# Decode attention with a Mish layer on one core: who issues the loads

## The chip, the cores and the metric

The kernel runs on one core of a Trainium2 chip. A core has a matrix engine (TensorE, PE), a vector engine (VectorE, DVE), an activation engine (ScalarE, ACT), a general engine (GpSimd, POOL) and a synchronising engine (SyncE, SP). Each runs its own stream of instructions; they wait for one another through semaphores. 16 DMA engines move data between the memory of the chip (HBM) and the on-chip memory (SBUF). PE writes to a second on-chip memory, PSUM.

The metric is the time of one execution on the device, in microseconds (us), as the median of several runs.

## The reference

For 8 batches with one new token each, a layer-normalised row goes through two branches, which are added to the input: attention over a cache of 8192 keys and values, with 32 query heads that share 8 key/value heads, and a dense layer with a Mish activation.

```python
xn = _layernorm(x, axis=-1)                               # x: 8 x 1 x 512
q = (xn @ wq).reshape(B, Sq, 32, 128).transpose(0, 2, 1, 3)
k = jnp.repeat(k_cache, 4, axis=1)                        # caches: 8 x 8 x 8192 x 128
v = jnp.repeat(v_cache, 4, axis=1)
p = _softmax(einsum("bhqd,bhkd->bhqk", q, k) * 128 ** -0.5)
a = einsum("bhqk,bhkd->bhqd", p, v).transpose(0, 2, 1, 3).reshape(B, Sq, 4096) @ wo
h = xn @ w1 + b1                                          # w1: 512 x 1792
sp = log1p(exp(-abs(h))) + where(h > 0, h, 0)
return x + a + (h * tanh(sp)) @ w2                        # w2: 1792 x 512
```

All data is float32. The two caches are 268 MB each, and each of their bytes is used once.

## The kernel before

The work is cut into 16 packs. A pack is two batches and two key/value heads. For each of its two batches the kernel loads one block of keys and one of values, 128 partitions by 64 KB, 8.39 MB each. So there are 32 K loads and 32 V loads (two V loads are cut into two pieces each). Beside them stand the weights: four loads of `wq`, three of `wo` and a last one in two parts, one of `w1`, and `w2` in three parts at the end. That makes 79 loads.

The loads go into three places in SBUF. `kva` holds V blocks (and at the start `w1` and the second K block), `kvb` holds K blocks (at the end a V block and `w2`), `kvw` holds `wq` or `wo`. `kvb` is a quarter larger than one block: two successive K blocks lie a quarter apart, and the 16 rounds of score matmuls run forward for one block and backward for the next. So the next K load overlaps only three quarters of the old block, and waits for 48 of its 64 matmuls.

For each batch of a pack, PE multiplies the queries with the K block (tile `c`, 64 matmuls), ACT copies the scores out of PSUM (`sc`), and PE gathers them by rows (`s`). After the second batch DVE takes the row maxima, ACT the exponentials, and DVE transposes and folds them into the weights `pt`. While the scores of pack p are worked on, PE multiplies the weights of pack p-1 with its V blocks (tile `o`, 64 matmuls), and DVE gathers the result (`os`).

The program is written once as a list of operations (class `Program`); who waits for whom is derived from the tiles that operations read and write. Each ordered pair of producer and consumer has a semaphore, with two further rules. A DMA counts as a producer of its own, named by its `stream` ("k", "v", "w" and so on). And `relay(engine, to, after)` puts a bare wait on an engine's stream that, once passed, tells another engine. PE, DVE and ACT run packs 1 to 15 as a loop; in each round they lower their semaphores again. SP and POOL run straight through.

The loads stand in one queue (`plan`, L499). `pump` (L479) issues from its head as long as the place is free; `release` (L491) frees a place, keeps the relay that tells of its last reader in `held`, and pumps again. All loads are DMAs on SP's stream, in this order: `wq`, `w1`, the first K block; then K and V in turn, with a weight now and then. SP waits for the place to be read, issues, and goes on to the next. PE waits for a load's own semaphore. The relays that tell SP stand on DVE for V blocks and weights (after the matmuls that read them), on ACT for the second K block and on POOL for `w1`. K loads wait for PE itself. All instructions carry line L383 of the code, where a helper records them; they are told apart by their tiles.

At the start POOL sets up an identity matrix and a few constants. After that it has only the relays of `w1`. At the end it clears the semaphores.

Of the kernel before, what the change touches and what calls it, by code (L numbers as in the profile page):

```python
# [59 lines left out]
W2R = G * FT // 2 * FP // P  # L60
FAR = 1e38


ENGINES = ("tensor", "vector", "scalar", "gpsimd", "sync")
LOOPED = ("tensor", "vector", "scalar")
FIRST, END = 1, PACKS
RARE = ("w",)
# [7 lines left out]
class Op:  # L75
    def __init__(self, engine, method, make=None, outs=(), ins=(), stream=None, to=None):
        self.engine, self.method, self.make = engine, method, make
        self.outs, self.ins, self.to = outs, ins, to
        self.who = stream or engine
        self.unit = 16 if stream else 1  # L80
        self.waits = []


class Engine:
# [25 lines left out]
class Program:  # L110
# [74 lines left out]
    def add(self, op, after=()):  # L185
        op.pack, op.seq = self.pack, len(self.ops)
        looped = self.zone == "loop"
        op.part = self.name if looped else None
        if op.who in RARE:
            op.part = op.who  # L190
        key = op.engine, self.zone, self.at if looped else 0
        start = self.starts[self.pack] if looped else 0
        number = self.numbers.get((*key, start), 0)
        self.numbers[(*key, start)] = number + 1
        op.place = (*key, number)
        op.n = self.count.get(op.who, 0)
        self.count[op.who] = op.n + 1
        know = self.know[op.engine]
        op.needs = [*after, *self.conflicts(op)]
        for other in op.needs:  # L200
            if know.get(other.who, -1) < other.n or op.method == "relay":
                giver = self.giver(op, other)
                self.learn(know, giver)
                op.waits.append(giver)
        assert op.who == op.engine or know.get(op.who, -1) == op.n - 1, op.who
        op.clock = dict(know)
        self.ops.append(op)
        if op.to:
            self.sends[op.place] = op.to
        for ap, writes in [(a, False) for a in op.ins] + [(a, True) for a in op.outs]:  # L210
            self.seen[ap.tensor.name][op.who, writes, self.region(ap)] = op
        return op
# [231 lines left out]
def kernel(  # L444
# [13 lines left out]
    prog = Program(nc)  # L458
    pe, dve, act, pool, sp = (getattr(prog, e) for e in ("tensor", "vector", "scalar", "gpsimd", "sync"))
# [13 lines left out]
    taken, landed, held = {}, {}, {}  # L473
# [25 lines left out]
    def plan(what, at, blocks, stream, part=(0, 1), lo=0):  # L499

        rows = rows_of(blocks)
        n = rows.shape[1]
        t = place[at][:, lo : lo + n]

        cols = slice(round(part[0] * n), round(part[1] * n))

        def load():
            sp.dma_start(t[:, cols], rows[:, cols], stream=stream, to="tensor", after=held.pop(at, ()))
            return t

        queue.append((what, at, load))
# [39 lines left out]
    for p in range(PACKS):  # L551
        for b in range(PB):
            plan_k(p, b)
            if (p, b) in between:
                what, i = between[p, b]
# [169 lines left out]
    def queries(w):  # L725

        for r in range(QR):
            for e in range(2):
                last = pe.matmul(
                    H[HE * e : HE * (e + 1), :],  # L730
                    xnT[:, r].rearrange("p g q -> p (g q)"),
                    w[:, r * BW + e * D : r * BW + (e + 1) * D],
                    start=(r == 0),
                    stop=(r == QR - 1),
                )
        read = prog.relay("vector", "sync", last)
        copies = Q * KR // DH
        qs, qt = wide, raw
        for g in range(copies):
            dve.tensor_scalar_mul(  # L740
                qs.rearrange("p (h r g i) -> p h r g i", h=REP, r=KR, g=copies)[:, :, :, g],
                H.rearrange("p (h i r) -> p h r i", h=REP, r=KR),
                DH**-0.5,
            )
        dve.transpose(qt, qs)
        dve.tensor_copy(
            qc,
            qt.rearrange("p (h r q) -> p h r q", h=REP, r=KR)[:, :, :, :B].rearrange(
                "p h r b -> p b r h"
            ),  # L750
        )
        prog.settle("vector")
        return read
# [15 lines left out]
    def scores(b, k, order, first=False):  # L769

        t = qT[:, b].rearrange("p r u h -> p r (u h)")
        for r in order:
            if first and r == order[KR // 2]:
                load_early()
            for c in range(2):
                last = pe.matmul(
                    C[b][HE * c : HE * (c + 1), :],
                    t[:, r],
                    k[:, r * BW + c * 512 : r * BW + (c + 1) * 512],
                    start=(r == order[0]),  # L780
                    stop=(r == order[-1]),
                )
        read = prog.relay("scalar", "sync", last) if first else None
        act.copy(sc, C[b])
        return read

# [152 lines left out]
    def outputs(w):  # L939

        for h in range(2):
            for r in range(OR):
                at = r * BW + h * D
                last = pe.matmul(
                    H[Q * r : Q * r + B, :],
                    oW[:, r, h, :],
                    w[:, at : at + D],
                    start=(h == 0),
                    stop=(h == 1),
                )  # L950
        read = prog.relay("vector", "sync", last)
        dve.tensor_add(acc, H, acc)
        return read

# [25 lines left out]
    def mish(w1_sb):  # L980


        hp = O[1][:, :FG]
        for g in range(G):
            pe.matmul(
                hp[Q * g : Q * g + B, :], gsel[:, g, :], b1_sb, start=True, stop=False
            )
        for r in range(W1R):
            for g in range(G):
                at = r * F // 2 + g % 2 * FG  # L990
                last = pe.matmul(
                    hp[Q * g : Q * g + B, :],
                    xw[:, r, g // 2, :],
                    w1_sb[:, at : at + FG],
                    start=False,
                    stop=(r == W1R - 1),
                )

        read = prog.relay("gpsimd", "sync", last)
        done = prog.relay("gpsimd", "vector", last)  # L1000
        h, a, z, z2 = (wide[:, i * 512 : i * 512 + FG] for i in range(4))
        dve.tensor_copy(h, hp, after=[done])


        dve.scalar_tensor_tensor(a, h, -1.0, h, op0=ALU.mult, op1=ALU.max)
        act.activation(z, a, AF.Exp, scale=-1.0)
        dve.tensor_mul(z2, z, z)
        m = a
        dve.tensor_single_scalar(m, h, 0.0, op=ALU.is_gt)

        one = acc[:, :FG]
        dve.tensor_scalar(one, z2, -1.0, 1.0, op0=ALU.mult, op1=ALU.add)
        dve.tensor_mul(one, one, m)
        t1 = m
        dve.tensor_add(t1, one, z2)
        t2 = z2
        dve.tensor_scalar(one, one, -1.0, 1.0, op0=ALU.mult, op1=ALU.add)
        dve.scalar_tensor_tensor(t2, z, 2.0, t1, op0=ALU.mult, op1=ALU.add)
        dve.scalar_tensor_tensor(t1, one, 2.0, t2, op0=ALU.mult, op1=ALU.add)
        dve.reciprocal(z, t1)  # L1020
        dve.tensor_mul(t1, t2, z)
        got = one
        half = FG // 2
        for e in range(2):
            dve.tensor_mul(
                got.rearrange("p (i a e l) -> p e a l i", a=2, e=2, i=W2R)[:, e],
                h[:, half * e : half * (e + 1)].rearrange("p (a l i) -> p a l i", a=2, i=W2R),
                t1[:, half * e : half * (e + 1)].rearrange("p (a l i) -> p a l i", a=2, i=W2R),
            )
        dve.transpose(aT.rearrange("p j q -> p (j q)"), got)  # L1030
        dve.memset(acc, 0.0)
        dve.tensor_copy(acc[:B, :], x_sb)
        return read
# [19 lines left out]
    read = queries(landed["wq", 0])  # L1053
    release(("wq", 0), read)
    expand(0)
    read = mish(landed["w1"])
    release("w1", read)

    for p in range(PACKS):
        prog.enter(p)  # L1060
        for b in range(PB):
            k = landed.pop(("k", p, b))
            n = PB * p + b - (p > 0)
            order = range(KR) if n % 2 == 0 else range(KR - 1, -1, -1)
            read = scores(b, k, order, first=(p, b) == (0, 1))
# [23 lines left out]
            if (p, b) in between:  # L1089
                w = landed.pop(between[p, b])  # L1090
                read = outputs(w) if b else queries(w)
                release(between[p, b], read)
            prog.part(None)
            if p > 0:
                last = values(b, landed.pop(("v", p - 1, b)))
                read = prog.relay("vector", "sync", last)
                gather(b)
                release(("v", p - 1, b), read)
            if b == 1:
# [9 lines left out]
    collect(2)  # L1109
    turning()  # L1110
    last = values(0, landed["v", p, 0])
    read = prog.relay("vector", "sync", last)
    gather(0)
    release(("v", p, 0), read)
    sums()
# [67 lines left out]
```

## Time and profile before

| | |
|---|---|
| median of 3 runs | 1303.72 us (1303.66 to 1303.83) |
| span of the profiled execution | 1302.2 us |
| what the runs' median has beside that span | 1.5 us |
| moved by DMA | 561.22 MB in 11554 packets |
| busy: PE, DVE, ACT, POOL | 67%, 30%, 9%, 0% |

The profile comes from one execution, whose own time is its span; the runs' median holds in addition what lies before the first and after the last instruction. In the rows an instruction is named by its engine, its operation and its tiles (output <- inputs), with `xN` for a group of N. "PEld" is the loading of weights into PE. "SPq", "POOLq" and "DVEq" are an engine's own sequencer: waits, and the issuing of DMAs. In brackets stands how long the engine had been idle before and what ended that. The chain of waits is followed back from the last instruction: start, duration, and what it was. A row by stage has start and end, length, busy time (and number of instructions) of PE, PEld, DVE, ACT and POOL, the clock granted to PE, the busy share of the 16 DMA engines and GB/s. A row of DMA issues ends with the median of us from issue to landing.

### The profile page before, as it was taken

The numbers are of one execution on the slowest core, as the hardware profiler recorded it, in microseconds if no ns is written. First come the engines' busy times: TensorE is split into PE (matmuls) and PEld (weight loads), VectorE is DVE, ScalarE is ACT, GpSimd is POOL, SyncE is SP. The second block draws the span as 40 slices with busy tenths as digits, with TensorE's granted clock in tenths as the row PEclk, the third lists the DMA queues.
The fourth block names the chain that finished last, engine by engine and source line by source line (L and its number), as shares of the span: only waits on it lengthen the run. The fifth ranks groups of instructions, "written<-read, shape, count | busy, mean of one in ns | idle before, by whom it ended". The sixth has DMA issues, their size and how long they took to land.

```text
span 1302.2 us, 11363 instructions
## 1 busy us (share of the span) xinstructions
PE 869.0 (67%) x4814; PEld 278.5 (21%) x4814; DVE 389.9 (30%) x597; ACT 122.2 (9%) x294; POOL 4.8 (0%) x10
## 2 busy tenths in 40 slices
PE   4786666766567665686656686666866656756568
PEld 1222112212112221122211222111221121212113
DVE  6350504305051230521405132052320515105061
ACT  1020202001020100200102020020100102001020
POOL 1000000000000000000000000000000000000000
PEclk9898789887799788897877897778877888878779
DMA  9999999999999999999999999999999999999998
GB/s 404 447 419 446 421 441 429 431 439 429 439 429 441 425 443 423 436 433 431 439 429 439 420 450 425 441 425 441 429 431 439 429 439 429 441 425 439 427 429 372
DMA packets 11554, 561.22 MB, mean 431 GB/s; under 512 B 1292, under 2 KB 1424, under 8 KB 1688
## 3 DMA queue, kind: packets, MB, share of 16 engines
q1 hardware_dynamic: 11520, 561.06, 99.7%
q8 instruction: 7, 0.11, 0.0%
q10 hardware_dynamic: 24, 0.02, 0.0%
q14 instruction: 3, 0.02, 0.0%
HBM read 561.01 MB, written 0.07 MB: 431 GB/s over the span
## 4 chain that ended last, share of the span: by engine, by line
DMA 61%; PE 31%; DVE 1%; issue 0%; SPq 0%; ACT 0%; DVEq 0%
DMA kvb<-in_kT 60%; PE c L383 29%; DMA kvb<-in_w 2%; PE o L383 1%; DVE raw L383 0%; DVE pt L383 0%; PE h L383 0%; DVE os L383 0%; DVE nm L383 0%; PE s L383 0%; PE m L383 0%; SPq L383 0%; ACT sc L383 0%; DVE acc L383 0%; DVE nr L383 0%
## 5 line engine op out<-in xcount | busy, mean ns | idle before, releaser
L383 PE MATMUL c<-kvb,qT 128*64 128x512 f32 x1984 | 497.7, 665 | 332.8 <-DMA kvb<-in_kT 332.2
L383 PEld LDWEIGHTS c<-kvb,qT 128*64 128x64 f32 x1984 | 160.8, 154 | 669.6 <-issue 459.4
L383 PE MATMUL o<-kva,pt 128*32 128x512 f32 x1984 | 238.0, 635 | 24.5 <-DMA kva<-in_v 24.1
L383 DVE TENSOR_REDUCE nm<-s 128x1 f32<-128x1024 f32 x16 | 19.6, 1225 | 437.0 <-PE s L383 437.0
L383 DVE STREAM_TRANSPOSE raw<-wide 128x2048 f32<-128x2048 f32 x36 | 125.5, 3485 | 19.5 <-ACT wide L383 17.7
L383 ACT COPY sc<-c 128x512 f32<-128x512 f32 x32 | 18.8, 586 | 979.1 <-PE c L383 979.1
L383 PEld LDWEIGHTS o<-kva,pt 128*32 128x32 f32 x1984 | 64.6, 116 | 189.1 <-issue 147.6
L383 ACT ACTIVATE wide<-s,nms 128x512 f32<-128x512 f32 x128 | 88.0, 688 | 130.4 <-DVE nms L383 66.9
L383 DVE TENSOR_TENSOR oT<-m,rt 128x16 f32 (+1 forms) x17 | 3.0, 175 | 229.6 <-PE m L383 229.6
L383 DVE TENSOR_SCALAR os<-o,isel 128x128 f32<-128x128 f32 x32 | 11.2, 350 | 151.1 <-PE o L383 151.1
L383 DVE TENSOR_TENSOR pt<-raw 64x256 f32<-64x256 f32 x128 | 53.6, 418 | 1.9
L383 DVE TENSOR_TENSOR qT<-qc,bsel 128x1024 f32<-128x1024 f32 x34 | 40.2, 1221 | 13.3 <-PE s L383 13.3
L383 PE MATMUL s<-sc,csel 64*128 64x512 f32 x128 | 37.1, 656 | 8.5 <-ACT sc L383 7.1
L383 DVE TENSOR_TENSOR raw<-raw 128x1024 f32<-128x1024 f32 x32 | 39.2, 1225 | 2.9 <-DVE raw L383 0.2
L383 DVE SCALAR_TENSOR_TENSOR os<-o,isel,os 128x128 f32<-128x128 f32 x96 | 33.6, 350 | 3.4
L383 ACT ACTIVATION_READ_ACCUMULATOR wide<-s,nms 128x1 f32 x128 | 24.7, 193 | 0.0
L383 PE MATMUL m<-hsel,os 128*128 128x8 f32 x66 | 12.7, 265 | 10.5 <-DVE lsel L383 10.5
L383 PE MATMUL m<-ident,nm 128*1 128x128 f32 x16 | 4.3, 270 | 21.6 <-DVE nm L383 21.6
L383 PE MATMUL h<-kvw,xnT 128*64 128x512 f32 x64 | 17.6, 700 | 0.0
L383 PE MATMUL c<-kva,qT 128*64 128x512 f32 x64 | 15.7, 652 | 2.1 <-DMA kva<-in_kT 2.1
L383 DVE TENSOR_SCALAR wide<-h 128x512 f32<-128x512 f32 x16 | 11.1, 691 | 19.9 <-PE h L383 19.5
L383 PEld LDWEIGHTS m<-hsel,os 128*128 128x128 f32 x66 | 10.1, 193 | 25.3 <-issue 12.2
(92 smaller groups left out, 162.1 us busy)
## 6 DMA issues: line engine op xcount, KB each, us to landing
kvw<-in_wq SPq DMA_DIRECT2D x4, 2048.0 KB, 30.3
kva<-in_v SPq DMA_DIRECT2D x2, 4096.0 KB, 21.6
kvw<-in_wo SPq DMA_DIRECT2D x3, 2048.0 KB, 30.4
kva<-in_v SPq DMA_DIRECT2D x1, 6144.0 KB, 24.3
kva<-in_w SPq DMA_DIRECT2D x1, 3584.0 KB, 15.8
kva<-in_v SPq DMA_DIRECT2D x1, 2048.0 KB, 28.8
kvb<-in_w SPq DMA_DIRECT2D x1, 2048.0 KB, 13.7
kvw<-in_wo SPq DMA_DIRECT2D x1, 1536.0 KB, 16.9
```

Of the source, the lines that this page charges most:

```text
L383: got = getattr(engine, o.method)(*args, **kw)
```

## The change

The first three loads (`wq`, `w1`, the first K block) stay on SP. The other 76 are issued on POOL's stream (`pool.dma_start`), where GpSimd's software writes the descriptors. Their semaphores go to SP instead of PE. Behind each of them SP gets a relay, the load's `proxy`: a wait for the landing that then tells PE. Whoever would have waited for such a load waits for its proxy. The relays that told SP that a place is free now tell POOL, on the same engines as before; the one for `w1` is left out, as POOL waits for PE's matmul itself.

```diff
+FIRST_LOADS = (("wq", 0), "w1", ("k", 0, 0))
+MORE = {}
...
@@ class Op
+        self.proxy = None
...
@@ Program.add
         for other in op.needs:
             if know.get(other.who, -1) < other.n or op.method == "relay":
+                if other.proxy and op.engine != other.proxy.engine:
+                    other = other.proxy
                 giver = self.giver(op, other)
...
@@ plan
         def load():
-            sp.dma_start(t[:, cols], rows[:, cols], stream=stream, to="tensor", after=held.pop(at, ()))
+            first = what in FIRST_LOADS
+            op = (sp if first else pool).dma_start(
+                t[:, cols],
+                rows[:, cols],
+                stream=stream,
+                to="tensor" if first else "sync",
+                after=held.pop(at, ()),
+                **({} if first else MORE),
+            )
+            if not first:
+                op.proxy = prog.add(Op("sync", "relay", to="tensor"), [op])
+                op.proxy.part = stream if stream in RARE else None
             return t
...
@@ queries, outputs, the body (V blocks)
-        read = prog.relay("vector", "sync", last)
+        read = prog.relay("vector", "gpsimd", last)
...
@@ scores
-        read = prog.relay("scalar", "sync", last) if first else None
+        read = prog.relay("scalar", "gpsimd", last) if first else None
...
@@ mish
-        read = prog.relay("gpsimd", "sync", last)
+        read = last
```

`MORE` is empty. What is loaded, into which place and in which order is the same.

More of the change, by code (lines that the diff above doesn't have):

```diff
@@ L950, in outputs @@
                 )
-        read = prog.relay("vector", "sync", last)
+        read = prog.relay("vector", "gpsimd", last)
         dve.tensor_add(acc, H, acc)
@@ L1095 @@
                 last = values(b, landed.pop(("v", p - 1, b)))
-                read = prog.relay("vector", "sync", last)
+                read = prog.relay("vector", "gpsimd", last)
                 gather(b)
@@ L1111 @@
     last = values(0, landed["v", p, 0])
-    read = prog.relay("vector", "sync", last)
+    read = prog.relay("vector", "gpsimd", last)
     gather(0)
```

## The prediction

> **What bounds the kernel now.** I read the page's head and chain first, then busy time by stage, then the chain in order of time and the issues on SP.
>
> ```profile
> span 1302.2 us, 11363 instructions
> PE 869.0 (67%) x4814; PEld 278.5 (21%) x4814; DVE 389.9 (30%) x597; ACT 122.2 (9%) x294; POOL 4.8 (0%) x10
> POOL 1000000000000000000000000000000000000000
> q1 hardware_dynamic: 11520, 561.06, 99.7%
> q10 hardware_dynamic: 24, 0.02, 0.0%
> DMA 61%; PE 31%; DVE 1%; issue 0%; SPq 0%; ACT 0%; DVEq 0%
> 76.00:115.00 39.00, 24.56 (x138) 8.26 (x138) 17.13 (x25) 6.82 (x17) 0.00 (x0) 0.88 1.01 435
> 115.00:1228.00 1113.00, 739.45 (x3928) 234.42 (x3928) 317.56 (x470) 103.66 (x252) 0.00 (x0) 0.83 1.00 433
> 1278.00:1302.00 24.00, 19.58 (x308) 9.33 (x300) 3.48 (x12) 0.41 (x2) 0.00 (x0) 1.00 0.83 346
> ```
>
> The last two numbers of a stage's row are the share of the 16 DMA engines and GB/s. From 115 to 1228 us the engines are full at 433 GB/s, and one queue, q1, moved 561.06 MB. The transfers are the bound; every other engine is below 70%. The chain's 31% of PE is only the way a load's release is found: a K load of 8.39 MB takes 8.39 / 433 = 19.4 us of the stream, yet the chain alternates so:
>
> ```profile
> 78.33 12.06 PE c L383 x48
> 90.41 24.71 DMA kvb<-in_kT
> ...
> 115.16 12.43 PE c L383 x48
> 127.61 26.21 DMA kvb<-in_kT
> ...
> 1268.08 9.36 PE o L383 x64
> ...
> 1277.46 0.03 DVEq L380
> ...
> 1277.51 0.33 SPq L383
> ...
> 1278.36 19.55 DMA kvb<-in_w
> 1297.91 0.04 issue
> 1297.95 1.87 PE h L383 x56
> ```
>
> A K load is released by 48 of 64 score matmuls and lands 24.71 us later at the least in the loop, 19.4 of them its own bytes. For the other 5.3 us it stands behind a V load, or in fixed latency. The smallest load of the trace bounds that latency:
>
> ```profile
> kvb<-in_kT SPq DMA_DIRECT2D x31, 26.1
> kva<-in_v SPq DMA_DIRECT2D x29, 31.5
> kvb<-in_w SPq DMA_DIRECT2D x1, 2048.0 KB, 13.7
> out<-acc SPq DMA_DIRECT2D x1, 64.0 KB, 1.5
> ```
>
> The store of 64 KB takes 1.5 us in all, so a K load has 5.3 - 1.5 = 3.8 us of cover before the stream runs dry; a typical V load has 31.5 - 19.4 - 1.5 = 10.6 us. This cover is what the change spends.
>
> **The change, part by part.** Of 79 loads on SP 76 move to GpSimd (POOL). Removed: 76 issues of 0.33 to 0.43 us on SP, about 26 us, none on the path except the two at 1277.51, and those stand under transfers already queued. The relay through POOL that told SP of the first gate matrix's last matmul goes too; POOL now waits for that matmul itself. Added: 76 issues on POOL, 76 waits on SP that pass a landing to PE. POOL is busy only in the first of 40 slices (ten instructions, 4.8 us), so behind a waiting issue stands only the next issue, as on SP before; behind a wait of SP stand its later waits and the output's store, and PE waits for them.
>
> Price of an issue on POOL: the trace has none. Its nearest rows are SP's 0.33 us and POOL's own short software work:
>
> ```profile
> L383 POOL COPY pt<-pt 8x512 f32<-8x512 f32 x2 | 2.2, 1086 | 5.2 <-DVE xnT L383 5.1
> L383 POOL MEMSET pt<- 128x2048 f32 x1 | 1.8, 1803 | 1.2 <-DVEq L380 1.2
> ```
>
> Bounds 0.3 to 1.8 us; I take 1.1. In the loop it costs 0.8 us more than SP, against 3.8 us of cover for K and 10.6 for V: nothing. At 1.8 us it still fits. Without the cover it would be 0.8 us on each of some 60 loads, 48 us.
>
> Price of the relay on SP: the hop PE, DVE, SP at the end shows it, 1268.08 + 9.36 = 1277.44 to 1277.51, 0.07 us for two hops; bounds 0.02 to 0.2, I take 0.1. In the loop it makes K's matmuls, and so the next release, 0.1 us late: covered. SP's waits stand in the order of the issues, and landings on one queue have kept that order, so no wait is held up by a later load. At the end the last landing (1297.91) is on the path: **+0.1 us**. The five last issues take 5 x 1.1 = 5.5 us on POOL for some 2 on SP; the last stands behind four loads and starts near 1296.7, 13 us after it is issued: nothing. The first of them lands after 13.7 us, 4.8 of its own bytes, so 7.4 us of cover.
>
> The place where two queues meet. q1 is SP's and q10 is ACT's (its 24 packets are the two small inputs), so POOL's loads will ride a queue of their own. Once, at the start, loads of both stand side by side:
>
> ```profile
> 1.65 0.42 SPq L383 DMA_DIRECT2D kvb<-in_kT  x1
> 27.71 0.33 SPq L383 DMA_DIRECT2D kva<-in_kT  x1
> 37.66 15.33 PE L383 MATMUL c<-kvb,qT 128*64 128x512 f32 x64 [10.07 <-DMA kvb<-in_kT]
> 49.61 0.33 SPq L383 DMA_DIRECT2D kvb<-in_kT  x1
> 53.74 1.13 PE L383 MATMUL s<-sc,csel 64*128 64x512 f32 x4 [0.75 <-ACT sc L383]
> 57.02 15.65 PE L383 MATMUL c<-kva,qT 128*64 128x512 f32 x64 [2.15 <-DMA kva<-in_kT]
> 65.84 7.24 SPq L383 DMA_DIRECT2D kva<-in_v  x2
> ```
>
> Today the second K load (27.71) waits behind the first (landed 37.6) and lands at 57.0; the third is released 11.95 us after the first landed (37.66 to 49.61) and then waits for the second's bytes. On a queue of its own the second need not wait. How the engines divide themselves no row tells. Bounds: in order of issue, the first is not delayed; newcomer first, it is delayed by all 19.4 us. I take the middle, alternate packets. With 1.2 us of the 1.5 us latency split evenly before and after the bytes, the second begins at 27.7 + 1.1 + 0.6 = 29.4; the first, whose bytes ended near 37.0, has 7.6 us left. A packet is 65.5 KB (8.39 MB in 128 rows), 2.4 us on one of 16 engines; three are left, two or three newcomers go between: 4.8 to 7.3 us, I take 6.0. The first K load then lands at 43.6, the third is released at 55.6 and starts at 57.3. The second's bytes still end at 57.02 - 0.6 = 56.4, the sum of both being the same: **0.9 us dry** (0 for a delay of 4.8, 2.5 for an even split of 7.6, 14.4 for 19.4). A dry stream is not won back, since it is full to the end.
>
> The Trainium skill ("DMA: Bandwidth & Descriptors", Queues, rings and completion order) has each DMA engine go round-robin over its queue rows, a packet at a time. By that rule the sum is the one just made; by today's trace, which has one full queue, it could be any in the bounds.
>
> What is late next: the score matmuls of the second K load start when PE has done the first (43.6 + 15.3, plus 2 us for the row sums as from 53.0 to 54.9), at 61.0 for 57.02, and what follows moves by 4.0 us. The fourth K load, released at 90.41 today, is released at 94.4 and starts at 96.1; the stream then has the third and the V load before it, 57.3 + 2 x 19.4 = 96.1. Cover of zero; bounds 0 to 1.5, **+0.5 us**. From there the loop's cover is back, as it is set by the 12.1 to 12.5 us of matmuls against 19.4 us of V.
>
> Sum: 0.9 + 0.5 + 0.1 = 1.5 us on a span of 1302.2, so 1303.7; the runs' median lies 1303.72 - 1302.2 = 1.5 us above the span, so **1305.2 us**, +0.12%. Own range: 1303.8 (all zero) to 1307.9 (2.5 + 1.5 + 0.2).
>
> **The rivals.**
>
> *Served in order* (or POOL's first issue so slow that the first K load is nearly through): only the relay remains, 1303.8. For it: no row shows two full queues sharing. Against it: none shows order either.
>
> *Newcomer first*: 14.4 us dry, 1303.7 + 14.5 = 1318.2. It decides above a delay of 5 us to the first K load. Against it: it needs an arbiter that prefers POOL's queue.
>
> *VectorE keeps POOL from writing.* In each pack the V load is issued into VectorE's longest run:
>
> ```profile
> 1179.45 1.23 DVE L383 TENSOR_TENSOR raw<-raw 128x1024 f32<-128x1024 f32 x1
> 1179.73 0.33 SPq L383 DMA_DIRECT2D kva<-in_v  x1
> ...
> 1183.84 3.61 DVE L383 STREAM_TRANSPOSE raw<-wide 128x2048 f32<-128x2048 f32 x1
> 1187.48 1.22 DVE L383 TENSOR_TENSOR raw<-raw 128x1024 f32<-128x1024 f32 x1
> 1188.74 1.72 DVE L383 TENSOR_TENSOR pt<-raw 64x256 f32<-64x256 f32 x4
> ...
> 1208.81 7.07 PE L383 MATMUL o<-kva,pt 128*32 128x512 f32 x64 [1.22 <-DMA kva<-in_v]
> ```
>
> This load lands 29.1 us after its issue, cover 29.1 - 19.4 - 1.5 = 8.2 us. Were POOL shut out until 1190.5, the issue would be 10.7 + 1.1 us late: 3.6 us dry, 15 times, 54 us, 1358. It decides where the delay passes 8.2 us. One instruction's delay (3.6 us) is covered, and K loads are issued with VectorE idle. The Trainium skill ("SBUF — State Buffer", Who interferes with whom) says that VectorE's copies and tensor_scalar between SBUF tiles, in a two-port mode, shut GpSimd out for a whole instruction, so that its descriptors are late. None of the rows above is of that kind, and by that rule the sum stays; the rule names the mechanism, the cover its price.
>
> *The stream is slower.* The stage at 435 GB/s and the loop's 433 differ by 0.46%, a bound for what overhead per packet this stream shows. If descriptors written by software cost as much again, 561.06 MB take 6.0 us longer: 1305.2 + 6.0 = 1311.2. The Trainium skill ("DMA: Bandwidth & Descriptors", Bandwidth) gives 425 GB/s for 16 MB issued from GpSimd; by it the stream would be 1.9% or some 24 us longer, an estimate.
>
> *The stream is faster* (the other side): the loop runs at the 435 of that stage, 6.0 us less, 1299.2. It needs today's loss to lie in how SP's queue is fed. Against it: share 1.00, large packets.
>
> *The change does nothing*: the loads stay on q1; 1303.7.
>
> **How the numbers follow.** Forecast 0.47; in order 0.16; slower stream 0.12; faster stream 0.09; newcomer first 0.08; VectorE 0.07; nothing 0.01. The range, 1300.0 to 1319.0, reaches to the newcomer and most of both stream cases and leaves out VectorE, the faster stream's end and the slower's, some 0.16. A measurement here tells 0.2% (2.6 us) from no change: below 1301.1 the faster stream, 0.09; above 1306.3 newcomer, VectorE, slower stream and a quarter of the forecast, 0.40; the rest 0.51.
>
> **What would show it.** Right: POOL's issues at some 1.1 us; the first K load landing near 43.6; a dip in GB/s near 56 us and full slices after it; 433 GB/s in the loop; K loads landing 25 to 27 us after issue. Wrong: GB/s in the loop off 433 by 2 or more, dips at each V load, the first K load at 37.6 or at 57, or a dry stretch before the last loads.

## The result and the profile after

The changed kernel takes 1315.69 us (median of 4 runs, 1314.29 to 1316.87) against 1303.69 us: 1.0092 of the time before, 95% interval 1.0077 to 1.0106. It is slower by 12 us. The profiled execution is the shortest of the four (1314.29 us); its span is 1313.0 us, 10.8 more than before.

From the page of the changed kernel: span, engines, queues, chain, and the two big groups of issues on POOL (after the bar: busy us, mean ns of one, idle before and what ended it).

```profile
span 1313.0 us, 11424 instructions
PE 869.6 (66%) x4814; PEld 279.3 (21%) x4814; DVE 390.0 (30%) x597; ACT 122.1 (9%) x294; POOL 45.0 (3%) x86
q0 software_dynamic: 10880, 546.84, 96.4%
q1 hardware_dynamic: 576, 14.22, 2.6%
DMA 65%; PE 32%; DVE 1%; issue 1%; ACT 0%; SPq 0%; POOL 0%; DVEq 0%; ACTq 0%
L389 POOL DMA_DIRECT2D kvb<-in_kT x30 | 15.8, 528 | 701.9 <-PE c L389 701.9
L389 POOL DMA_DIRECT2D kva<-in_v x33 | 17.4, 528 | 476.5 <-DVEq L386 458.3
```

The change does what it says: 546.84 MB went over a new queue, q0. The engines are as busy as before, and an issue costs 0.53 us of POOL. The stages of the changed kernel show where the time went:

```profile
37.60:57.00 19.40, 14.76 (x60) 4.74 (x62) 3.34 (x7) 0.00 (x0) 0.53 (x1) 0.77 1.00 419
57.00:76.00 19.00, 17.48 (x80) 5.28 (x76) 1.22 (x1) 1.17 (x2) 1.05 (x2) 1.00 0.91 394
76.00:115.00 39.00, 26.20 (x139) 8.72 (x138) 17.72 (x24) 6.81 (x17) 1.01 (x2) 0.78 0.82 348
115.00:1228.00 1113.00, 741.54 (x3928) 235.40 (x3928) 318.18 (x472) 103.53 (x252) 32.73 (x63) 0.83 1.00 433
```

The kernel before has, from 57 to 76 us:

```profile
57.00:76.00 19.00, 16.85 (x69) 5.27 (x69) 1.35 (x2) 0.59 (x1) 0.00 (x0) 0.91 1.00 434
```

In the long loop the stream runs at 433 GB/s, as before. Nearly all of the loss lies before 115 us: 348 GB/s where there were 435, 394 where there were 434. (A stage's row counts a packet where it starts, so the GB/s of a short stage is rough; the landings below give the sizes.) The instructions there, in order of time (PE's row names what ended its idle time):

```profile
27.95 0.67 POOL L389 DMA_DIRECT2D kva<-in_kT  x1 [11.97 <-PE o L389]
42.24 16.10 PE L389 MATMUL c<-kvb,qT 128*64 128x512 f32 x64 [14.99 <-DMA kvb<-in_kT]
55.23 0.53 POOL L389 DMA_DIRECT2D kvb<-in_kT  x1 [26.61 <-PE c L389]
60.15 13.95 PE L389 MATMUL c<-kva,qT 128*64 128x512 f32 x64
67.54 0.53 POOL L389 DMA_DIRECT2D kva<-in_v  x1 [11.78 <-PE c L389]
74.45 0.53 POOL L389 DMA_DIRECT2D kva<-in_v  x1 [6.38 <-ACTq L386]
88.43 16.89 PE L389 MATMUL c<-kvb,qT 128*64 128x512 f32 x64 [9.24 <-SPq L386]
102.19 0.53 POOL L389 DMA_DIRECT2D kvb<-in_kT  x1 [27.21 <-PE c L389]
```

The view of a tile, limited to one load's issue, gives its time to landing. For the loads issued at 27.95, 55.23, 67.54, 74.45 and 102.19, in this order:

```profile
DMA to landing us min/median/max: 28.7/28.7/28.7
DMA to landing us min/median/max: 23.3/23.3/23.3
DMA to landing us min/median/max: 20.7/20.7/20.7
DMA to landing us min/median/max: 23.5/23.5/23.5
DMA to landing us min/median/max: 23.6/23.6/23.6
```

So the second K load lands at 56.7, the third at 78.5, the two pieces of V at 88.2 and 98.0, the fourth K load at 125.8. On a full stream 8.39 MB follow in 19.4 us. Between 56.7 and 78.5 there are 2.4 us too many, between 98.0 and 125.8 there are 8.4 too many; in sum 10.8, the whole loss of this execution. There the stream runs dry: some or all of the DMA engines have nothing queued.

The second gap is the large one, and its cause stands in the row at 88.43. The third K load has been there since 78.5, and PE has stood idle since 79.2 (9.24 us), yet its matmuls start at 88.43, 0.2 us after the landing of the first piece of V. PE waited for the wrong load.

### The profile page after: what moved, and what is told of

It is laid out like the page before. It is cut to its first block, busy times and chain, and to the rows that moved or that the text cites. A ratio compares the mean times of both kernels' runs of the same rounds, so it can differ in the third digit from the quotient of the medians.

```text
span 1313.0 us, 11424 instructions
## 1 busy us (share of the span) xinstructions
PE 869.6 (66%) x4814; PEld 279.3 (21%) x4814; DVE 390.0 (30%) x597; ACT 122.1 (9%) x294; POOL 45.0 (3%) x86
## 3 DMA queue, kind: packets, MB, share of 16 engines
q0 software_dynamic: 10880, 546.84, 96.4%
## 4 chain that ended last, share of the span: by engine, by line
DMA 65%; PE 32%; DVE 1%; issue 1%; ACT 0%; SPq 0%; POOL 0%; DVEq 0%; ACTq 0%
DMA kvb<-in_kT 62%; PE c L389 31%; DMA kva<-in_v 2%; DMA kvb<-in_w 1%; DVE raw L389 1%; PE o L389 1%; DVE pt L389 0%; ACT wide L389 0%; PE s L389 0%; PE h L389 0%; DVE os L389 0%; DVE nm L389 0%; ACT sc L389 0%; PE m L389 0%; SPq L389 0%
## 5 line engine op out<-in xcount | busy, mean ns | idle before, releaser
L389 PE MATMUL o<-kva,pt 128*32 128x512 f32 x1984 | 238.5, 636 | 22.8 <-SPq L386 22.4
L389 DVE TENSOR_TENSOR qT<-qc,bsel 128x1024 f32<-128x1024 f32 x34 | 40.2, 1222 | 19.0 <-PE s L389 19.0
L389 POOL DMA_DIRECT2D kvb<-in_kT x30 | 15.8, 528 | 701.9 <-PE c L389 701.9
L389 POOL DMA_DIRECT2D kva<-in_v x33 | 17.4, 528 | 476.5 <-DVEq L386 458.3
L389 ACT ACTIVATION_READ_ACCUMULATOR wide<-s,nms 128x1 f32 x128 | 24.7, 193 | 0.0
```

The costliest lines, as they stand in the source:

```text
L389: got = getattr(engine, o.method)(*args, **kw)
```

## The theories

*Counter theory.* Before, PE waited on one semaphore for each stream of loads. Now all landings but those of weights come to PE from SP, over one semaphore that counts them. PE runs packs 1 to 15 as one loop, so a wait has the same count in each pack, relative to what the rounds before took off, and it must be the largest that any pack needs. In packs 2 to 15 the first K load of a pack is third among the landings not yet taken off. In pack 1 it is second, as the first V load, whose two pieces move all later landings on by one, only comes behind it. But the loop waits for three, and third in line is the first piece of that V load. So the wait is false in one pack only, and the fourth K load is released late by it.

*Queue theory.* The loss comes from the second K load sharing the engines with the first (landed 42.2 for 37.6), and what that delays.

## The experiments

**A counter for each stream.** The relay counts as its load's stream and not as SP:

```diff
-                op.proxy = prog.add(Op("sync", "relay", to="tensor"), [op])
+                relay = Op("sync", "relay", to="tensor")
+                relay.who = "got_" + stream
+                op.proxy = prog.add(relay, [op])
+                prog.know["sync"][relay.who] = op.proxy.n
```

> The changed kernel, but SP counts its landings separately for each stream of loads (K, the two pieces of the first V load, V, weights), so that PE waits for the one load it needs. Counter theory (in the changed kernel PE's wait for the third K load is a wait for three landings on one counter, the third of which is the first piece of the first V load): the third K load's score matmuls start near 80 us instead of 88.4, the fourth K load is issued near 93 instead of 102.2, the dry stretch from 95 to 103 us is gone, and about 2 us remain from the first dry stretch: 1305.5 us (1304.5 to 1306.5). Queue theory (all of the loss comes from the second K load sharing the DMA engines with the first, which lands 4.6 us late): no change, 1315.7 us.

Measured: 1308.10 us (1305.98 to 1308.49), 1.0029 [1.0019, 1.0039]. Its timeline:

```profile
44.29 16.28 PE L389 MATMUL c<-kvb,qT 128*64 128x512 f32 x64 [17.53 <-DMA kvb<-in_kT]
57.46 0.53 POOL L389 DMA_DIRECT2D kvb<-in_kT  x1 [29.34 <-PE c L389]
81.90 16.25 PE L389 MATMUL c<-kvb,qT 128*64 128x512 f32 x64 [0.49 <-PEq L366]
95.02 0.53 POOL L389 DMA_DIRECT2D kvb<-in_kT  x1 [17.80 <-PE c L389]
```

PE no longer waits for a load there, and the fourth K load is issued 7 us earlier than in the changed kernel although the first K load was later still. The counter theory holds, for the larger part of the loss; 4.4 us are left. The remainder was larger than I expected: in this execution the first K load came at 44.3, and the third landed 24.2 us after the second (80.9 and 56.7), 4.8 too many. The nine runs fall into two groups, 1305.98 to 1306.20 and 1307.99 to 1308.49. The first K load delayed by one packet more (2.4 us) would make just that, but only one execution of each kernel has a trace, so this is argued.

**The second K load on SP**, the one counter kept:

```diff
-FIRST_LOADS = (("wq", 0), "w1", ("k", 0, 0))
+FIRST_LOADS = (("wq", 0), "w1", ("k", 0, 0), ("k", 0, 1))
...
-        read = last
+        read = prog.relay("gpsimd", "sync", last)
```

> The changed kernel with the second K load issued by SP too, so that the first K load is alone on its queue; the one counter stays. Counter theory: the first K load lands at 37.6 us again, the third K load on POOL's queue meets the second instead and delays it to about 61; the first piece of V lands near 86, PE starts the third K load's matmuls then, the fourth K load is issued near 99, dry for some 5 us: 1309 us. Queue theory: the first K load is not delayed, so the loss is gone but for 1 us: 1304.7 us.

Measured: 1311.15 us (1311.03 to 1311.59), 1.0057 [1.0042, 1.0072]. Its timeline:

```profile
59.40 15.65 PE L389 MATMUL c<-kva,qT 128*64 128x512 f32 x64 [3.20 <-DMA kva<-in_kT]
86.17 16.32 PE L389 MATMUL c<-kvb,qT 128*64 128x512 f32 x64 [6.09 <-SPq L386]
99.36 0.53 POOL L389 DMA_DIRECT2D kvb<-in_kT  x1 [23.43 <-PE c L389]
```

The false wait is there, as foretold (86, 99), with the first K load back at 37.6. The queue theory falls as the account of the whole loss. The price is 2 us above my 1309: the fourth K load lands at 122.6 for 115.1, 7.5 us, because a load on a dry stream takes 23.2 us, of which more below.

**Both edits.**

> Both edits: the second K load on SP and a counter for each stream. Counter theory: no wait for a load that isn't needed; the second K load lands near 61 us for 57, the fourth K load is issued near 95 to 96, at the end of what is queued, so 0 to 1 us dry: 1304.6 us (1303.8 to 1305.5). Queue theory: 1304.7 us as well. This run tells what is left of the price when both are taken away: issuing on POOL and the relay on SP, 0.1 to 1 us.

Measured: 1305.63 us (1304.63 to 1308.70), 1.0018 [1.0008, 1.0027], just above the range foretold and with a spread of 4 us. In the traced execution, the shortest (span 1303.2, 1.0 above before), the second K load, delayed by the third on the other queue, is late by 2 us, and the fourth is issued at 92.5:

```profile
59.17 15.65 PE L389 MATMUL c<-kva,qT 128*64 128x512 f32 x64 [3.60 <-DMA kva<-in_kT]
80.39 15.28 PE L389 MATMUL c<-kvb,qT 128*64 128x512 f32 x64 [0.50 <-PEq L366]
92.54 0.53 POOL L389 DMA_DIRECT2D kvb<-in_kT  x1 [16.84 <-PE c L389]
```

**The counter without POOL's loads.** All loads stay on SP, as before the change; POOL passes their landings on, over one counter (the proxy and its use as in the change; arguments left out are marked):

```diff
-            sp.dma_start(t[:, cols], rows[:, cols], stream=stream, to="tensor", after=held.pop(at, ()))
+            first = what in FIRST_LOADS
+            op = sp.dma_start(..., to="tensor" if first else "gpsimd", ...)
+            if not first:
+                op.proxy = prog.add(Op("gpsimd", "relay", to="tensor"), [op])
+                op.proxy.part = stream if stream in RARE else None
```

> The kernel before, all loads on SP as there, but POOL passes the landings of all loads but the first three on to PE, over one counter: no load is issued by POOL and no second queue exists. Counter theory: the third K load's matmuls wait for the first piece of V (issued at 65.8, landed near 86.5), the fourth K load is issued near 100 for 90.4, the stream is dry for some 6 us: 1309.7 us (1308.5 to 1311). Queue theory: nothing shares, so 1303.8 us.

Measured: 1311.16 us (1310.02 to 1311.40), 1.0054 [1.0039, 1.0070]. The median lies just above the range foretold.

```profile
86.11 16.87 PE L388 MATMUL c<-kvb,qT 128*64 128x512 f32 x64 [8.47 <-POOLq L385]
99.58 0.33 SPq L388 DMA_DIRECT2D kvb<-in_kT  x1
76.00:115.00 39.00, 25.88 (x138) 8.61 (x137) 16.99 (x25) 6.81 (x17) 0.00 (x0) 0.82 0.84 351
```

No load on POOL, no second queue, and the hole is the same: 351 GB/s from 76 to 115 us. The false wait alone costs 7.5 us.

**The same with a counter for each stream** (the first experiment's edit on top, with POOL in place of SP):

> All loads on SP as in the kernel before, POOL passes the landings on, with a counter for each stream. Beside the run with one counter (1311.2 us) it takes away the one counter alone, with no second queue in either. Counter theory: 1303.8 us, the whole 7.5 us back; if the relay itself costs something on the path, more than that.

Measured: 1303.75 us (1303.63 to 1303.95), 1.0001 [0.9992, 1.0010]. All of it comes back. Passing a landing on costs 0.1 us in the median, which is not clear of the spread; the prediction had 0.1.

**The price of a restart by itself.** With counters by stream, the second K load on POOL waits until the first has landed, so the queues do not meet, and the stream runs dry once:

```diff
+            if what == ("k", 0, 0):
+                told.append(prog.relay("sync", "gpsimd", op))
...
-                after=held.pop(at, ()),
+                after=[*held.pop(at, ()), *(told if what == ("k", 0, 1) else [])],
```

(The first K load is passed on by SP here, too.)

> The kernel with a counter for each stream, and the second K load on POOL now waits until the first K load has landed: no two full queues meet, but the stream runs dry once, at 37.6 us. This measures the price of a restart by itself. Dear restart (an 8.39 MB load on a dry stream lands 23.2 to 23.6 us after its issue, as the traces so far have it): the second K load is issued near 37.9 and lands near 61.2 for 57.0, everything after it 4.2 us later: 1308.0 us (1307 to 1309). Cheap restart (1.5 us beside its own 19.4, as I had it in the prediction): it lands near 58.8, 1305.6 us.

Measured: 1308.40 us (1308.39 to 1309.09), 1.0039 [1.0025, 1.0052].

```profile
37.64 0.67 POOL L389 DMA_DIRECT2D kva<-in_kT  x1 [21.66 <-SPq L386]
60.10 16.45 PE L389 MATMUL c<-kva,qT 128*64 128x512 f32 x64 [5.01 <-SPq L386]
```

On a dry stream the load lands 22.4 us after its issue: 3.0 us beside its bytes, where I had set 1.5. The whole comes to what the dear restart foretold, though the load itself landed some 1 us earlier than that; the next K load, issued at 50.11, is 4.3 us late (80.6 for 76.3). The view of the DMA engines from 34 to 42 us, in 40 slices of 0.2 us, shows part of the 3.0 us; a packet counts in the slice where it starts:

```profile
DMA  7700000000000000000000000999097000000000
```

The first packets of the load start at 39.0, 1.4 us after its issue, and the last engine begins by 40.2, up to 2.6 us after it.

**The cover of a K load in the loop.** On top of both edits, 20 short memsets on POOL before the issue of each K load from the third on:

```diff
+            if what[0] == "k" and what[1] > 0:
+                for _ in range(20):
+                    pool.memset(spare, 0.0, after=prog.conflicts(Op("gpsimd", "dma_start", outs=[t[:, cols]])))
```

> The kernel with both edits (second K load on SP, a counter for each stream), with 20 short memsets on POOL, each behind the last, between the wait for the place and the issue of every K load from the third on: the issue comes 4 to 6 us later. This tests the cover of a K load in the loop. Prediction's cover (3.8 us): nearly hidden, a few us in all, 1306 to 1320 us. Small cover (24.7 - 23.3 = 1.4 us at the least and 3 at the most, as a restart costs 3.8 us and not 1.5): each K load without a weight load ahead is some 2 us late, 25 of them: 1350 us (1330 to 1370).

Measured: 1357.47 us (1356.47 to 1358.47), 1.0412 [1.0393, 1.0431]. Its group of memsets, its loop and one K load of its chain:

```profile
L389 POOL MEMSET spare<- 128x128 f32 x600 | 123.9, 206 | 775.6 <-PE c L389 742.7
115.00:1228.00 1113.00, 717.59 (x3792) 228.22 (x3792) 308.69 (x456) 102.95 (x251) 141.80 (x600) 0.83 0.98 417
717.72 22.31 DMA kvb<-in_kT
```

A row of 20 takes 5.2 us, and the stream falls to 417 GB/s. The time from issue to landing of the K loads from 115 to 1228 us, with both edits alone and then with the memsets:

```profile
DMA to landing us min/median/max: 24.9/25.9/31.0
DMA to landing us min/median/max: 21.9/22.3/26.1
```

So of the 5.2 us of delay 3.6 are hidden in the median and 1.6 are not; on 30 K loads that is 48 us of the 52 measured (1357.47 against 1305.63). The cover is 3.6 us in the median and 3.0 at the least, where the prediction had 3.8 at the least. My expectation that 3.8 would nearly hide the delay did not follow from it: 5.2 - 3.8 = 1.4 us on 30 loads is 42 us. The run gives the size of the cover; it does not show the smaller cover of 1.4 to 3 us that I had set against it, though the time lay in the range foretold for that.

**Small pieces, on each queue.** POOL's loads, with counters by stream, and then the kernel before, with pieces of 16 KB for rows of 64:

```diff
-MORE = {}
+MORE = {"max_dma_last_dim": 16384}
```

> The kernel with a counter for each stream, with POOL's rows cut into pieces of 16 KB, so that its packets are a quarter of SP's in size and four times as many. If the queues alternate packet for packet, the second K load gets only a fifth of the engines while the first is in flight: the first K load lands at 38 to 40 us instead of 42 to 44, and the third is released before the queue is empty. If they share by bytes, the first K load lands near 43 as before. For the loop: no overhead per packet gives 433 GB/s and 1304 us; overhead per packet as bounded in the prediction (0.46% for one of 65.5 KB) gives 427 to 428 GB/s and 1320 us.

> The kernel before with all of SP's loads cut into pieces of 16 KB: the same question for the hardware queue. No overhead per packet: 1303.7 us. Overhead as bounded in the prediction: 427 to 428 GB/s in the loop, 1320 us. If the two kinds of queue differ in it, this run and the one with 16 KB pieces on POOL differ in the loop's GB/s.

Measured: 1317.81 us (1317.77 to 1318.01), 1.0109 [1.0093, 1.0124], on POOL, and 1317.99 us (1317.88 to 1318.03), 1.0109 [1.0094, 1.0125], on SP. The first three rows are from POOL's kernel, the last from SP's.

```profile
38.91 15.39 PE L389 MATMUL c<-kvb,qT 128*64 128x512 f32 x64 [12.33 <-DMA kvb<-in_kT]
51.20 0.75 POOL L389 DMA_DIRECT2D kvb<-in_kT  x1 [23.02 <-PE c L389]
115.00:1228.00 1113.00, 743.20 (x3904) 235.25 (x3908) 316.25 (x466) 103.66 (x252) 44.03 (x61) 0.83 1.01 428
```

```profile
115.00:1228.00 1113.00, 739.87 (x3918) 234.53 (x3922) 316.12 (x466) 103.66 (x252) 0.00 (x0) 0.83 1.01 428
```

Two things follow. The queues alternate by packets: with POOL's packets a quarter of SP's the first K load lands at 38.9, 1.2 us late, and not at 42 to 44. And a packet costs the same on both queues, 428 GB/s on either.

**Only the one load that meets another in small pieces**, with counters by stream:

```diff
-                **({} if first else MORE),
+                **({"max_dma_last_dim": 16384} if what == ("k", 0, 1) else {}),
```

> The changed kernel with a counter for each stream, and only the second K load (the one that meets the first on the other queue) cut into pieces of 16 KB; 75 loads on POOL go as they are. If the two costs found are all there is (the wait for a load that isn't needed, and the first K load's delay by whole packets of 65.5 KB), the first K load lands near 39 us, the third is released near 51, nothing runs dry: 1304.0 us (1303.7 to 1304.5), the kernel before plus the relay and the overhead of one load in small pieces. If issuing on POOL costs something of its own, 1305 us or more.

Measured: 1304.07 us (1303.59 to 1306.72, 11 runs), 1.0008 [0.9999, 1.0017]; the trace has

```profile
38.80 15.39 PE L389 MATMUL c<-kvb,qT 128*64 128x512 f32 x64 [12.26 <-DMA kvb<-in_kT]
51.08 0.53 POOL L389 DMA_DIRECT2D kvb<-in_kT  x1 [22.95 <-PE c L389]
115.00:1228.00 1113.00, 741.13 (x3928) 235.14 (x3928) 317.52 (x470) 103.65 (x252) 32.86 (x62) 0.83 1.00 433
```

With the two costs taken away and 76 loads still on POOL, the kernel is as fast as before, in the median. So the changed kernel's 12.0 us divide into 7.6 for the one counter (1315.69 to 1308.10) and 4.0 for the queues that meet (1308.10 to 1304.07); 0.4 are left. Three of the 11 runs lie at 1305.7 to 1306.7, though, which no run of the kernel before does.

**The same with 1.0 us more before each K load** (four memsets of the kind above).

> The kernel with a counter for each stream and the second K load in pieces of 16 KB, with four short memsets on POOL (1.0 us) between the wait for the place and the issue of every K load from the third on. This tells what is behind the runs of that kernel that lie 2 to 3 us above its median. Cover of 2.5 us (loop's 24.7 us at the least from issue to landing against 22.2 on a dry stream in the run with 5 us of delay): 1.0 us is hidden, 1304 to 1305 us and no more high runs than before. At the edge already (the high runs are K loads that come too late): the median rises by 3 us or more and most runs are high.

Measured: 1306.84 us (1304.13 to 1308.17, 11 runs), 1.0020 [1.0011, 1.0029]. The median rises by 2.8 us and six of 11 runs lie at 1306.8 or above, so a delay of 1 us is not wholly hidden. That speaks for K loads that in some executions come a little too late as the cause of the high runs. The trace taken here (1305.56 us) has the loop at 433 GB/s and shows no late load, so it is not shown.

No kernel here beat the kernel before.

## Why the prediction was right or wrong

The time lay in the range (1300.0 to 1319.0), but by luck: the forecast, 1305.2 and no change, did not come true, and the range reached so far up only for a rival that did not happen. Newcomer first had 1318.2; the first K load would have landed at 57 and landed at 42.2.

**The step that failed**: "SP's waits stand in the order of the issues, and landings on one queue have kept that order, so no wait is held up by a later load." That is true on SP, where the prediction looked. It is false one hop on, at PE: merging the streams into one counter turned PE's wait for the third K load into a wait for the first piece of V. The rows: 88.43 for a load that landed at 78.5. Alone it costs 7.4 us (1311.16 against 1303.75). In the sum the stretch before the fourth K load ("what is late next") stood as 0.5 us, without this wait; it measured 8.4. The sign "full slices after it" failed with it: 348 GB/s from 76 to 115 us. The code held all that was needed: PE's loop, the semaphores that it lowers in each round and the split V load all stand in the description of the kernel.

**Queues that meet**: mechanism right. "Alternate packets" was the choice between the bounds, and the runs with small pieces confirm it. The first K load was delayed by 4.6 us (6.6 in another kernel's trace) for 6.0. That the third was issued at 55.2 for 55.6 is in part chance: the first landed 1.4 us earlier than foretold, and its 48 matmuls took 13.0 us for 12.0. The Trainium skill ("DMA: Bandwidth & Descriptors", Queues, rings and completion order) has the engines go round-robin over the queues, a packet at a time. The traces agree, if one piece of a row is taken as a packet: 4.6 to 6.6 us of delay with pieces of 64 KB, 1.2 with 16 KB.

**The dry stretch after it**: 2.4 us for 0.9. The term mis-sized is the restart: I took the 1.5 us of a 64 KB store for the latency of any load. A load of 8.39 MB on a dry stream landed 21.9 to 23.6 us after its issue, 2.5 to 4.2 beside its bytes. The cover of a K load, worked out with the same 1.5, came out nearly right: 3.0 us at the least and 3.6 in the median for 3.8.

**POOL's issue**: 0.53 us (0.67 the first time) for 1.1, within the bounds. **The relay**: nothing clear of the spread (1303.75 against 1303.64 with POOL passing on all landings but three); SP's passing on was not run by itself. **The loop**: hidden, right in the traces, with 433 GB/s and K loads at 24.7 us and more.

**The rivals.** VectorE did not keep POOL from its work: all issues but the first take 527 to 541 ns, those into VectorE's long run too, and the V loads of the loop land 31.2 us after their issue for 31.5 before. None of these issues fell on a STREAM_TRANSPOSE in the changed kernel's trace, so it does not show that case. The stream is neither slower nor faster by who writes the descriptors: 433 GB/s, and with 16 KB pieces 428 on both queues. My bound for the overhead per packet was a fair one: it foretold 1320 for those, 1318 was measured. The 425 GB/s that the Trainium skill ("DMA: Bandwidth & Descriptors", Bandwidth) gives for 16 MB did not appear: 433 in the loop.

## What to carry to other kernels

When a relay stands in for several producers, ask not only in which order it waits but how its consumer counts: a loop with one wait for all rounds takes the largest count, and a first round that is arranged otherwise then waits for a load it does not need. When a second queue is opened, look for the moment at which both are full; there the load that is needed first is delayed by whole packets of the other, and cutting the newcomer alone into small pieces takes most of the delay away (1.1 us left of 4.6 to 6.6 here). Measure the slack of a prefetch against a load on a dry stream, not against the smallest transfer.

## What was unexpected in the hardware

A restart is dear: 21.9 to 23.6 us for 19.4 us of bytes, on either queue (23.2 us for SP's load at 99.58). In the run that waits for the first K load 1.4 us pass before the first packet, and the engines do not begin together; why stays open. Small pieces on a dry stream were not tried.

The overhead per packet is visible: cutting rows of 64 KB into four adds 24448 packets over 16 engines, 1528 each, and 14.3 us: 9.4 ns a packet.

Six of the nine kernels with loads on POOL vary by 2 to 4 us from run to run. The other three stay within 0.8, in four or five runs each: the second K load on SP with the one counter, the wait for the first K load, and 16 KB pieces on POOL. The three with all loads on SP and nothing waited for in vain stay within 1.0. So loads on POOL alone do not make the spread. One part can be the number of packets that go between. Another can be a K load that comes too late; but the kernel that waits for the first K load has the same time to landing in the loop (25.9 us in the median) and did not vary. Neither is shown.
